# Reordering an attention-plus-gated-MLP kernel around its exponentials: layer norm statistics further ahead, the row-sum matmul moved to a later step, and seven eighths of the last output product moved forward

## The chip, the cores and the metric

One NeuronCore of a Trainium2 chip. The metric is the device time of one execution, in microseconds (us). Runs of this one-core program agree with the others of the same kernel within about 0.5%. The span of a profile is the time from the first to the last instruction of one profiled execution; it is some 2 us shorter than the time.

## The reference, cut to what matters

```python
x  = A_x                                   # 1 x 2048 x 512, bf16
xn = layernorm(x)
A  = softmax(q @ k.T * 16**-0.5) @ v, all heads, @ wo     # 32 heads of 16
B  = (relu(xn @ W_gate) * (xn @ W_up)) @ W_down           # hidden width 1792
out = x + A + B
```

Layer norm, attention and the gated MLP read the same normalized tensor. The softmax needs 32 x 2048 x 2048 exponentials.

## The kernel before

The kernel has three stages.

*Layer norm.* 16 tiles of 128 rows. For each tile VectorE sums the row and ScalarE sums the squares; for each chunk of four tiles a chain of tiny VectorE operations and one square root give mean and reciprocal deviation. Each tile is normalized in two passes on VectorE, transposed on PE through PSUM, copied to SBUF, and its V projection follows at once.

```python
for c in range(NQC):
    for i in range(4):
        t = 4 * c + i
        d_xn = ln_apply(t)                      # VectorE, two passes
        tk = transpose_tile3(t, d_xn)           # PE
        if prev is not None:
            pt_, ptk = prev
            evac_tile(pt_, ptk)                 # ScalarE for even tiles, VectorE for odd ones
            proj_V(pt_)                         # PE, then a copy on ScalarE
        prev = (t, tk)
        if i == 1 and c + 1 < NQC:
            for tt in range(4 * (c + 1), 4 * (c + 1) + 4):
                ln_stats(tt)                    # sum on VectorE, squares on ScalarE
        if i == 2 and c + 1 < NQC:
            rr = ln_finish_stats(4 * (c + 1), 4 * (c + 1) + 4)
```

*Attention.* A unit is one group of four heads with one chunk of 512 queries; there are 32 units, and 683 steps run through all of them. In each step PE makes three blocks of scores, ScalarE makes one exponential over 128 x 1536 of them, and PE multiplies earlier exponentials with V into one accumulator bank, psA (the row sums come from a column of ones in V). With what is left of a step PE does two matmuls of background work (the projections and the whole MLP, all through one bank, psX), or, when none is left, two idle "filler" matmuls. At a unit's end the accumulator is copied to `Tsb`, a matmul with a selection matrix (`sel`) spreads the row sums over the partitions, and VectorE and POOL divide.

```python
def emit_sel(u, dT):
    while st["psX_open"]:
        emit_bg_step()                          # finish the open background product in one burst
    pS = mm(psX[:], lhsT=sel[:], rhs=Tsb[:], start=True, stop=True,
            waits=[dT, g_sel] + psX_waits(), stream=s_peX)
    dL = vop(lambda: dve.tensor_copy(Lsb[:], psX[:]), waits=[pS, st["L_free"]])
    ...                                         # four reciprocal pieces, one per later step

for a in range(A_total + 1):
    ...                                         # scores, exponentials, PV; a unit's end emits the copy to Tsb
    emit_recip_piece()
    if pending_sel:
        emit_sel(*pending_sel.popleft())        # in the same step as the copy
        k = PE_BUDGET
    else:
        try_outproj()
        k = bg_advance(PE_BUDGET)
    for _ in range(PE_BUDGET - k):
        emit_filler()
```

*End.* After the last unit: copy, row sums, four reciprocals, one division on POOL, then the output product of the last 512 queries, 32 matmuls, and residual, and four writes.

The softmax here doesn't subtract the row's maximum and nothing guards it: scores larger than these inputs give would overflow.

## Time and profile before

| | before |
|---|---|
| time, median | 1099.17 us (16 runs, 1097.01 to 1100.65) |
| span of the profile | 1095.4 us |
| first exponential starts | 66.09 us |
| last exponential ends | 1075.73 us |
| time covered by exponentials | 981.0 us |
| idle of ScalarE between exponentials | 28.6 us |
| from the last exponential to the end | 19.7 us |

The span is the sum of four of these numbers: 66.1 before the first exponential, 981.0 covered by them, 28.6 between them, 19.7 after the last. Each is read from one profiled execution; that of the kernel before took 1097.41 us, 1.8 less than the median. The lines of the profile behind them stand in the prediction. In a row of the view in order of time the columns are start, length, engine, source line, operation, what is written and read, how many instructions were merged, and in brackets the idle time of the engine before it and what ended that. PE is the matmul engine (PEld its weight loads), DVE is VectorE, ACT is ScalarE, POOL is GpSimd.

### The profile page before, as it was taken

What the parts mean: (1) busy time and instruction counts of PE and PEld (TensorE: products, weight loads), DVE (VectorE), ACT (ScalarE), POOL (GpSimd) and SP (SyncE); (2) the same over time, 40 slices, a digit from 0 to 9 for tenths busy, and PEclk for the clock granted to TensorE, in tenths of its full rate; (3) what the DMA queues carried; (4) which work ended last, traced back from release to release, by engine and by line L of the source; (5) the groups of instructions that cost most, each with busy time, mean ns of one, the idle gap of its engine ahead of it and who ended that gap; (6) DMA issues with size and microseconds to landing.
All of it is one profiled execution on the core that took longest, in us unless ns stands there. A gap on an engine that the chain in (4) does not pass through costs nothing.

```text
span 1095.4 us, 13671 instructions
## 1 busy us (share of the span) xinstructions
PE 877.7 (80%) x5688; PEld 234.1 (21%) x5758; DVE 323.1 (30%) x498; ACT 1011.6 (92%) x746; POOL 49.2 (4%) x52
## 2 busy tenths in 40 slices
PE   3588888888888888888888888877778877777775
PEld 2222222222222222222222222221212222212211
DVE  5433323432332323443123342210112211101112
ACT  4479999999999999999999999999999999999992
POOL 1000010000000000000000000000000000000000
PEclk9789999999999999999999999999999999999998
DMA  9000000000000000000000000000000000000000
GB/s 335 1 1 1 1 7 15 1 1 1 1 1 1 20 1 1 1 1 1 1 1 1 21 1 1 1 1 1 1 1 1 20 1 1 1 1 1 1 1 20
DMA packets 8749, 12.67 MB, mean 12 GB/s; under 512 B 752, under 2 KB 7152, under 8 KB 8688
## 3 DMA queue, kind: packets, MB, share of 16 engines
q1 hardware_dynamic: 8688, 11.80, 3.1%
q8 instruction: 45, 0.74, 0.3%
q14 instruction: 16, 0.13, 0.0%
HBM read 9.70 MB, written 2.10 MB: 11 GB/s over the span
## 4 chain that ended last, share of the span: by engine, by line
ACT 50%; issue 22%; PE 18%; DVE 8%; DMA 1%; SPq 0%; POOLq 0%; POOL 0%; ACTq 0%
ACT PT L511 48%; PE psX L157 9%; PE psS L157 5%; PE psA L157 5%; DVE rl L576 2%; DVE Tsb L554 2%; DVE Lsb L564 1%; DMA W<-in_A_wqkv_dram 1%; ACT junk L216 1%; DVE hT L704 1%; DVE KTx L444 1%; DVE gl L686 1%; ACT Vsb L314 0%; DVE xpb L723 0%; DVE KTc L652 0%
## 5 line engine op out<-in xcount | busy, mean ns | idle before, releaser
L511 ACT ACTIVATE PT<-psS,negshift 128x1536 bf16<-128x1536 f32 (+1 forms) x683 | 981.0, 1606 | 33.4 <-PE psA L157 20.3
L157 PE MATMUL psS<-QT,KTx 32*128 32x512 bf16 x2048 | 268.5, 386 | 125.8 <-ACT PT L511 122.9
L157 PE MATMUL psA<-PT,Vsb 128*17 128x512 bf16 x2048 | 270.4, 386 | 0.5 <-ACT PT L511 0.5
L157 PEld LDWEIGHTS psS<-QT,KTx 32*128 32x128 bf16 x2048 | 66.5, 91 | 460.3 <-ACT PT L511 410.8
L157 PE MATMUL psA<-zmov,wfill 128*32 128x512 bf16 x462 | 138.0, 380 | 0.0
L554 DVE COPY Tsb<-psA 128x512 f32<-128x512 f32 x32 | 22.1, 692 | 318.3 <-PE psA L157 318.3
L576 DVE RECIPROCAL rl<-Lsb 128x128 f32<-128x128 f32 x128 | 113.5, 924 | 1.1
L157 PEld LDWEIGHTS psA<-PT,Vsb 128*17 128x17 bf16 x2048 | 64.0, 87 | 157.0 <-issue 155.6
L584 POOL TENSOR_TENSOR OT<-Tsb,rl 128x512 bf16<-128x512 f32 x32 | 40.6, 1268 | 1017.7 <-DVE rl L576 959.1
L157 PE MATMUL psX<-xnT,wu 128*128 128x512 bf16 x209 | 64.6, 384 | 7.7 <-DVE gl L686 2.7
L157 PE MATMUL psX<-xnT,wg 128*128 128x512 bf16 x205 | 64.0, 386 | 8.5 <-DVE hT L704 3.2
L686 DVE TENSOR_SCALAR gl<-psX 128x512 bf16<-128x512 f32 x56 | 38.5, 688 | 95.7 <-PE psX L157 95.6
L157 PE MATMUL psX<-wd,hT 128*128 128x512 bf16 x210 | 63.7, 384 | 3.3 <-issue 1.9
L704 DVE TENSOR_TENSOR hT<-psX,gl 128x512 bf16<-128x512 f32 x56 | 38.3, 684 | 88.4 <-PE psX L157 88.3
L157 PE MATMUL psX<-Tsb,sel 128*128 128x512 f32 x64 | 36.4, 652 | 27.2 <-DVE Tsb L554 15.0
L157 PEld LDWEIGHTS psA<-zmov,wfill 128*32 128x32 bf16 x462 | 40.3, 96 | 21.7
L157 PE MATMUL psX<-xnT,W 128*128 128x512 bf16 x104 | 33.7, 402 | 3.7 <-DVE KTc L652 1.4
L157 PE MATMUL psX<-W,OT 128*128 128x512 bf16 x94 | 30.0, 402 | 7.7 <-POOL OT L584 6.1
L564 DVE COPY Lsb<-psX 128x512 f32<-128x512 f32 x32 | 22.1, 692 | 40.6 <-PE psX L157 40.6
L723 DVE TENSOR_TENSOR xpb<-psX,xpb 128x512 bf16<-128x512 f32 x16 | 11.0, 690 | 77.7 <-PE psX L157 77.7
L157 PE MATMUL psS<-ident,xn 128*128 128x128 bf16 x64 | 8.8, 282 | 24.6 <-DVE xn L260 24.6
L603 DVE TENSOR_TENSOR ostage<-psX,xpb 128x512 bf16<-128x512 f32 x12 | 8.3, 692 | 52.8 <-PE psX L157 52.8
(72 smaller groups left out, 240.6 us busy)
## 6 DMA issues: line engine op xcount, KB each, us to landing
xpb<-in_A_x_dram SPq DMA_DIRECT2D x4, 512.0 KB, 5.5
wg<-in_B_W_gate_dram SPq DMA_DIRECT2D x1, 1792.0 KB, 14.1
wu<-in_B_W_up_dram SPq DMA_DIRECT2D x1, 1792.0 KB, 17.3
wd<-in_B_W_down_dram SPq DMA_DIRECT2D x1, 1792.0 KB, 21.0
W<-in_A_wqkv_dram SPq DMA_DIRECT2D x1, 1536.0 KB, 10.3
out_dram<-ostage SPq DMA_DIRECT2D x3, 512.0 KB, 3.0
W<-in_A_wo_dram SPq DMA_DIRECT2D x32, 16.0 KB, 1.7
out_dram<-ostage SPq DMA_DIRECT2D x4, 128.0 KB, 1.7
```

The costliest lines, as they stand in the source:

```text
L157: ins = pe.matmul(out_ap, lhsT=lhsT, rhs=rhs, start=start, stop=stop, **kw)
L216: a2 = aop(lambda: act.activation(junk[:], xt, ACTF.Square, accum_out=stats[:, 1, t:t + 1]), waits=[xload[t // 4], act_last[0]])
L444: tk = vop(lambda: dve.tensor_scalar(KTx[:, b, :], KTc[:, t8, :], msk[:, 0:1], None, op0=ALU.mult), waits=w)
L511: tk = aop(lambda: act.activation(PT[:, slot:slot + cnt, :].rearrange("p a q -> p (a q)"), psS[:, rb * 512:(rb + cnt) * 512], ACTF.Exp, bi ...
L554: dT = vop(lambda: dve.tensor_copy(Tsb[:], psA[:]), waits=[pv_tick, st["Tsb_free"]])
L564: dL = vop(lambda: dve.tensor_copy(Lsb[:], psX[:]), waits=[pS, st["L_free"]])
L576: dR = vop(lambda: dve.reciprocal(rl[:, k * wdt:(k + 1) * wdt], Lsb[:, k * wdt:(k + 1) * wdt]), waits=[dL, st["rl_free"] if k == 0 else None])
L584: gO = gop(lambda: pool.tensor_tensor(OT[:, g, :], Tsb[:], rl[:], ALU.mult), waits=w)
L603: d = vop(lambda: dve.tensor_tensor(ostage[:, tt, :], psX[:], xpb[:, tile, :], ALU.add), waits=[tk, xpb_ready[tile], out_dma_ticks[-1] if ...
L686: d = vop(lambda: dve.tensor_scalar(gl[:], psX[:], 0.0, None, op0=ALU.max), waits=[tk, bst["gl_free"]])
L704: d = vop(lambda: dve.tensor_tensor(hT[:, fc, :], psX[:], gl[:], ALU.mult), waits=w2)
L723: d = vop(lambda: dve.tensor_tensor(xpb[:, tile, :], psX[:], xpb[:, tile, :], ALU.add), waits=[tk, xload[c], ln_all_dve, ln_all_act])
```

## The change

It has three parts, one for each place where ScalarE is not making exponentials. In the layer norm, the statistics run two chunks ahead, one tile per iteration, the chain is cut in two around the square root, all transposed tiles are copied by VectorE, the square-root table is loaded at the start, and the setup on POOL is reordered. At a unit's end, the row-sum matmul is held back to a later step, when its operand has been copied and the bank psX is closed, and no burst is made. At the end, seven of the eight head groups of the last output product are summed beforehand into `oacc` with the residual, and the last group is divided and multiplied in four pieces.

```diff
@@ layer norm @@
-                if t % 2 == 0:
-                    e = aop(lambda: act.activation(xnT[:, :, t * 128:(t + 1) * 128], tp3, ACTF.Copy),
-                            waits=[tk, act_last[0]])
-                    act_last[0] = e
-                else:
-                    e = vop(lambda: dve.tensor_copy(xnT[:, :, t * 128:(t + 1) * 128], tp3), waits=[tk])
+                e = vop(lambda: dve.tensor_copy(xnT[:, :, t * 128:(t + 1) * 128], tp3), waits=[tk])
...
             for t in range(4):
                 ln_stats(t)
-            rr = ln_finish_stats(0, 4)
+            a3 = ln_chain_part1(0, 4)
+            if NQC > 1:
+                for t in range(4, 8):
+                    ln_stats(t)
+            rr = ln_chain_part2(0, 4, a3)
...
-                    if i == 1 and c + 1 < NQC:
-                        cn = c + 1
-                        for tt in range(4 * cn, 4 * cn + 4):
-                            ln_stats(tt)
-                    if i == 2 and c + 1 < NQC:
-                        rr = ln_finish_stats(4 * (c + 1), 4 * (c + 1) + 4)
-                        for tt in range(4 * (c + 1), 4 * (c + 1) + 4):
-                            r_ready[tt] = rr
+                    if c + 2 < NQC:
+                        ln_stats(4 * (c + 2) + i)
+                    if c + 1 < NQC:
+                        if i == 1:
+                            pend_a3 = ln_chain_part1(4 * (c + 1), 4 * (c + 1) + 4)
+                        if i == 2:
+                            rr = ln_chain_part2(4 * (c + 1), 4 * (c + 1) + 4, pend_a3)
+                            ...
@@ a unit's end @@
-                while st["psX_open"]:
-                    emit_bg_step()
+                assert not st["psX_open"]
...
-                if pending_sel:
+                if pending_sel and not st["psX_open"] and fix_at[0] < a:
                     emit_sel(*pending_sel.popleft())
                     k = PE_BUDGET
                 else:
-                    try_outproj()
-                    k = bg_advance(PE_BUDGET)
-                for _ in range(PE_BUDGET - k):
+                    if not pending_sel:
+                        try_outproj()
+                        try_preout()
+                    k = bg_advance(PE_BUDGET, allow_new=not pending_sel or fix_at[0] == a)
+                for _ in range(0 if fix_at[0] == a else PE_BUDGET - k):
                     emit_filler()
@@ the end @@
+            def last_piece(u, k, dR):
+                c_ = slice(k * 128, (k + 1) * 128)
+                ot_piece[k] = gop(lambda: pool.tensor_tensor(OT[:, g_of(u), c_], Tsb[:, c_], rl[:, c_], ALU.mult),
+                                  waits=[dR, st["rl_free"]])
...
+            def step_preout(qc, tt):
+                ...                             # groups 0 to 6 into psX, then
+                d = vop(lambda: dve.tensor_tensor(oacc[:, tt, :], psX[:], xpb[:, tile, :], ALU.add),
+                        waits=[tk, xpb_ready[tile]])
...                                              # the final product then takes group 7 alone and adds oacc
```

Left out of the diff: the setup on POOL in its new order and the table preload, the declarations of `oacc` and `junkb1`, the two halves of the statistics chain (their operations are unchanged), and the bookkeeping that starts the early output product two steps after the seventh group is divided.

## The prediction

> **What bounds the kernel now.** I read the page first (busy shares, then the costliest groups), then ScalarE's instructions in order of time with what ended each idle stretch, then all engines in order of time in three places: the layer-norm stage, one unit end of the attention loop, the end. A unit is one group of four heads with one chunk of 512 queries; there are 32.
>
> ```profile
> PE 877.7 (80%) x5688; PEld 234.1 (21%) x5758; DVE 323.1 (30%) x498; ACT 1011.6 (92%) x746; POOL 49.2 (4%) x52
> L511 ACT ACTIVATE PT<-psS,negshift 128x1536 bf16<-128x1536 f32 (+1 forms) x683 | 981.0, 1606 | 33.4 <-PE psA L157 20.3
> ```
>
> ScalarE is the bound, through 683 exponentials that cover 981.0 us. The change touches none of them, so the span can fall only where ScalarE is not doing exponentials: before the first (it starts at 66.09), in 33.4 us of idle time before them, and after the last (it ends near 1075.7; the span is 1095.4). Of the 33.4, 4.83 lie before the first, so 28.6 us are stalls inside the loop: 1075.7 - 66.1 = 1009.6 = 981.0 + 28.6.
>
> ScalarE in order of time shows where: runs of 21 or 22 exponentials, one unit long, with a stall between. In the stretch where the background work has run out the stalls repeat as 0.55, 0.56, 0.20; earlier many are 1.2 to 2.1. One of the small ones, all engines:
>
> ```profile
> 889.77 0.39 PE L157 MATMUL psS<-QT,KTx 32*128 32x512 bf16 x3 [0.29 <-ACT PT L511]
> 890.09 0.09 PEld L157 LDWEIGHTS psA<-PT,Vsb 128*17 128x17 bf16 x2 [0.23 <-issue]
> 890.53 0.69 DVE L554 COPY Tsb<-psA 128x512 f32<-128x512 f32 x1 [24.08 <-PE psA L157]
> 891.27 1.12 PE L157 MATMUL psX<-Tsb,sel 128*128 128x512 f32 x2 [0.79 <-DVE Tsb L554]
> 892.33 0.39 PE L157 MATMUL psS<-QT,KTx 32*128 32x512 bf16 x3
> 893.13 4.40 ACT L511 ACTIVATE PT<-psS,negshift 128x1536 bf16<-128x1536 f32 x3 [0.55 <-PE psA L157]
> ```
>
> The row-sum matmul (sel) is next in PE's order, so PE stands through the copy of the accumulator, spends 1.06 us on it, and the next scores begin at 892.33, 2.56 after the last instead of about 1.43. The exponential follows its scores by at least 0.44 (923.05 to 923.49 in another unit end). The 2 us stalls have one thing more: PE first finishes the open background product in one burst (seven matmuls from 256.65 and then a copy out) ahead of sel.
>
> The layer-norm stage:
>
> ```profile
> 32.05 0.17 DVE L223 TENSOR_SCALAR stats<-stats 128x4 f32<-128x4 f32 x1 [5.34 <-ACT junk L216]
> 33.46 0.20 ACT L235 ACTIVATE stats_b<-stats_b 128x4 bf16<-128x4 bf16 x1 [0.76 <-DVE stats_b L233]
> 34.56 0.61 PE L157 MATMUL psS<-ident,xn 128*128 128x128 bf16 x4 [5.07 <-DVE xn L260]
> 47.84 0.61 PE L157 MATMUL psS<-ident,xn 128*128 128x128 bf16 x4 [5.07 <-DVE xn L260]
> ```
>
> Each chunk of four tiles takes 13.3 us (21.3, 34.56, 47.84), because the squares of the next chunk stand in ScalarE's queue behind copies out of PSUM, VectorE's statistics chain stands behind the squares, and the tiles stand behind that. PE is idle 5 us per chunk.
>
> The end:
>
> ```profile
> 1078.85 3.39 DVE L576 RECIPROCAL rl<-Lsb 128x128 f32<-128x128 f32 x4
> 1082.31 1.26 POOL L584 TENSOR_TENSOR OT<-Tsb,rl 128x512 bf16<-128x512 f32 x1 [28.70 <-DVE rl L576]
> 1084.21 3.19 PE L157 MATMUL psX<-W,OT 128*128 128x512 bf16 x7 [6.12 <-POOL OT L584]
> 1087.19 5.42 PE L157 MATMUL psS<-W,OT 128*128 128x512 bf16 x24
> 1092.65 0.69 DVE L624 TENSOR_TENSOR ostage<-psS,xpb 128x512 bf16<-128x512 f32 x1 [1.04 <-PE psS L157]
> ```
>
> Everything here is serial, and 32 output matmuls hang on the last unit although only 4 of them read it.
>
> **The Trainium skill.** "TensorE: Matmul & The Clock Gate", Part 1, says the PE clock is halved until about 3.4 us of sustained activity, and again after an idle window of that length. The trace agrees: four projection matmuls take 1.87 us after each 5 us idle stretch (15.43, 21.87, 35.12) and 1.04 once PE has worked on (27.27, 40.55). The same page's queue depths call ScalarE and VectorE strict FIFO; the 5 us idle stretches are what that costs here. "ScalarE: Activation LUTs", What ACT_TABLE_LOAD costs, gives about 1283 ns for a load; the trace has 1.28 us at 0.73, 7.79 and 59.98. It gives 186 ns + 0.833 ns per element for an activation with immediates, 613 ns for 512; the trace has 0.60 for the copies, against 0.42 for the same copy on VectorE.
>
> **The change, part by part.**
>
> (1) *Layer norm.* Preloading the square-root table removes the load at 7.79, but that ended at 9.07, before the chain that it would delay (9.12): worth 0. The reordered POOL setup still has the identity by about 6 us, needed at 12: worth 0. Statistics now run two chunks ahead, one tile per step, so nothing waits for squares. Four reductions (2.46 us) come before the first tile: first transposes near 12.6 instead of 10.4, but the weights land at 13.1, so only about 1.2 us of it counts, V of tile 0 at 14.4. Then VectorE sets the pace: apply 0.65 and copy out 0.42 per tile, reduction 0.62 per tile in the first two chunks, statistics chain 7 x 0.20 + 0.2 = 1.6 in the first three. With about 0.05 more for the copies and starts: 8.2 + 8.2 + 5.7 us. In the last chunk PE paces at about 1.2 to 1.25 per tile (transposes at 54.70 and 55.89 in the old one, warm), 5.0. From the first apply at 11.85 that ends at about 39; allow 1.5 for the slow clock at the start. The last V product then starts near 41 instead of 58.24. I book 16 us rather than 17, since nothing has shown yet that PE stays at full clock at 60% load. The tail of this stage (key mean, first keys and queries, 7.85 us from that V product to the first exponential) is unchanged: first exponential at 50.
>
> (2) *Unit ends.* Sel moves to a later step, when the copy is done and psX is closed; no burst, and at the step of the fixup no filler waits for the copy. Sel now costs PE its 1.06 in a step that otherwise takes scores 0.32, PV up to 0.43 and a switch 0.23: 2.05 from one score start to the next, 2.15 or 2.25 if psX is just being copied out. Plus 0.44 gives at most 2.7, and the exponential is due two periods, 2.85, after the former score start. So the stall vanishes with 0.15 to 0.35 to spare. The next PV needs the accumulator copy: copy ends 0.75 + 0.69 after the fixup step's scores, PV comes 1.43 + 0.32 after: 0.3 to spare. Left of 28.6: 1.6 that are no unit ends (0.70 at the start, 0.70 near 356 to 362, 0.21 at 615) and an allowance of 2: 3.6 left, 25 saved.
>
> (3) *The end.* Seven eighths of the last output product plus the residual go into oacc in place of fillers. Steps: fix of unit 30 at step 668, start at 670, 28 matmuls at two per step through 683, the last step: they just fit. The final path: reciprocals to 1082.24 as before; a POOL piece of 128 columns about 0.5 (a 128x128 POOL operation took 0.54), so the last at 1082.8; four single matmuls; four adds on VectorE from 1082.3 at 0.70 each to 1085.1, instead of 1093.34. Saved 8.2, and the last write follows as before.
>
> Sum: 16 + 25 + 8.2 = 49.2; 1098.3 - 49.2 = 1049.
>
> **Rivals.** (a) *PE stays cold in the layer norm.* 16 tiles at 2.28 us from 14.4 would end near 51: 7 to 8 us saved instead of 16, time 1058. For: 60% load with a gap per tile. Against: gaps of 1 us from 25 to 28 did not slow it. (b) *The unit-end stall only moves.* Sel still takes PE 1.06, and if score starts slip past 2.4 or VectorE delays the copy, each unit keeps 0.2 to 0.3: 32 x 0.25 = 8 us, time 1057. Against: the 0.20 stall came at a spacing of 2.57 and fits 2.57 + 0.44 - 2.85 = 0.16. (c) *The early output product misses its slots* by a late sel of unit 30: then a burst after the loop, or the old ending, losing 2 to 8 us. (d) *Nothing gained*, background work being the real bound: no, from about 740 on PE runs fillers.
>
> **Range and chances.** Layer norm 8 to 18, loop 20 to 26.5, end 5 to 8.7; not all bad together: 1043 to 1058. Faster by over 2% (below 1076.8) needs 21.5 of 49: even the loop alone, or its low end with a little of the rest, does that. Faster 0.97, within 2% 0.025, slower 0.005.
>
> **What will show it.** First exponential near 50 (55 to 58: rival a, with 1.87 us projections throughout). Exponential busy still about 981. Idle before exponentials inside the loop 2 to 6 us; 0.2 after every unit end says (b). Sel with no wait on Tsb. From last exponential to end about 11.5 us instead of 19.7; four single output matmuls. Wrong altogether if the exponentials lengthen, or if ScalarE begins to wait for PE in the middle of units.

## The result

The changed kernel takes 1039.35 us (median of 8 runs, 1038.67 to 1041.3) against 1099.17; the ratio is 0.9461, with a 95% interval of 0.9451 to 0.947. A ratio here is the mean time of one kernel's fast runs over that of the other's of the same rounds, so it is not quite the ratio of the two medians. Between the medians 59.8 us are saved, between the two profiled executions below 58.2, since the one of the kernel before was faster than its median. The output is correct.

| us | before | after | saved | predicted |
|---|---|---|---|---|
| before the first exponential | 66.1 | 46.2 | 19.9 | 16 |
| idle between exponentials | 28.6 | 2.1 | 26.5 | 25 |
| covered by exponentials | 981.0 | 977.7 | 3.3 | 0 |
| after the last exponential | 19.7 | 11.2 | 8.5 | 8.2 |
| span | 1095.4 | 1037.2 | 58.2 | 49.2 |

The profile after, from the page: busy shares, and the group of the exponentials (count, busy time and mean length of one, then idle time before them and what ended it).

```profile
PE 855.4 (82%) x5595; PEld 224.3 (22%) x5669; DVE 327.3 (32%) x510; ACT 1002.4 (97%) x738; POOL 49.7 (5%) x55
...
L538 ACT ACTIVATE PT<-psS,negshift 128x1536 bf16<-128x1536 f32 (+1 forms) x683 | 977.7, 1948 | 7.0 <-PE psS L159 7.0
```

ScalarE is now busy 97% of the span. Of the 7.0 us of idle before exponentials 4.83 lie before the first one. The mean length is no measure of speed: it went up from 1606 to 1948 ns, while the same 683 cover less time. A listed length of an instruction runs into its successor's, and more so the less the queue pauses.

ScalarE in order of time, rows with a pause ahead of them:

```profile
54.41 279.17 ACT L538 ACTIVATE PT<-psS,negshift 128x1536 bf16<-128x1536 f32 x195 [0.36 <-PE psS L159]
333.79 244.83 ACT L538 ACTIVATE PT<-psS,negshift 128x1536 bf16<-128x1536 f32 x171 [0.20 <-PE psS L159]
578.83 389.37 ACT L538 ACTIVATE PT<-psS,negshift 128x1536 bf16<-128x1536 f32 x272 [0.20 <-PE psS L159]
```

Where the kernel before paused after every 21 or 22 exponentials, there are now runs of 195, 171 and 272. Three rows give the pitch: (389.37 - 244.83) / (272 - 171) = 1.431 us per exponential. The same pitch comes out before: its runs of 22 and 21 took 31.59 and 30.16. So the exponentials are no faster; there are only fewer interruptions. (The prediction names longer exponentials as a sign of being wrong altogether; by the pitch they are not longer.)

A unit's end with background work, all engines (weight loads left out):

```profile
80.34 0.39 PE L159 MATMUL psS<-QT,KTx 32*128 32x512 bf16 x3 [0.19 <-ACT PT L538]
...
80.66 0.60 PE L159 MATMUL psA<-PT,Vsb 128*17 128x512 bf16 x5
...
81.19 1.13 PE L159 MATMUL psX<-Tsb,sel 128*128 128x512 f32 x2
...
82.25 0.39 PE L159 MATMUL psS<-QT,KTx 32*128 32x512 bf16 x3
```

The row-sum matmul waits for nothing here; the spacing of the scores is 1.91 us (82.25 - 80.34) where it was 2.56, and ScalarE runs on through it. The prediction had allowed 2.05 to 2.25.

The layer norm, VectorE alone, one tile and the start of the next:

```profile
19.46 0.34 DVE L261 TENSOR_SCALAR xc<-xpb,stats 128x512 bf16<-128x512 bf16 x1
19.84 0.35 DVE L264 TENSOR_SCALAR xn<-xc,stats 128x512 bf16<-128x512 bf16 x1
20.11 0.41 DVE L296 COPY xnT<-psS 128x512 bf16<-128x512 bf16 x1
20.45 0.67 DVE L218 TENSOR_REDUCE stats<-xpb 128x1 f32<-128x512 bf16 x1
21.04 0.34 DVE L261 TENSOR_SCALAR xc<-xpb,stats 128x512 bf16<-128x512 bf16 x1
```

No row has a bracket: VectorE never pauses here. A tile takes 1.58 us from start to start, although the four lengths add up to 1.77. A chunk takes 7.8 us (tile 0 is begun at 11.63, tile 4 at 19.46) instead of 13.3. The last V product starts at 38.33 instead of 58.24.

The end:

```profile
1029.47 3.39 DVE L617 RECIPROCAL rl<-Lsb 128x128 f32<-128x128 f32 x4
1030.50 0.45 POOL L607 TENSOR_TENSOR OT<-Tsb,rl 128x128 bf16<-128x128 f32 x1 [25.16 <-DVE rl L617]
...
1032.77 0.63 DVE L691 TENSOR_TENSOR ostage<-psX,oacc 128x512 bf16<-128x512 f32 x1
...
1033.32 1.87 DVE L691 TENSOR_TENSOR ostage<-psS,oacc 128x512 bf16<-128x512 f32 x3
```

The pieces are divided while later reciprocals run, and the adds follow the last reciprocal without a pause. The early output product found its slots.

### The profile page after: what moved, and what is told of

Its sections match the earlier page's. It is cut to its first block, busy times and chain, and to the rows that moved or that the text cites. A ratio compares the mean times of both kernels' runs of the same rounds, so it can differ in the third digit from the quotient of the medians.

```text
span 1037.2 us, 13490 instructions
## 1 busy us (share of the span) xinstructions
PE 855.4 (82%) x5595; PEld 224.3 (22%) x5669; DVE 327.3 (32%) x510; ACT 1002.4 (97%) x738; POOL 49.7 (5%) x55
## 4 chain that ended last, share of the span: by engine, by line
ACT 48%; issue 27%; PE 17%; DVE 6%; DMA 0%; DVEq 0%; ACTq 0%
ACT PT L538 48%; PE psX L159 7%; PE psS L159 5%; PE psA L159 5%; DVE rl L617 1%; DVE Lsb L597 1%; DVE stats L218 1%; DVE hT L776 1%; DVE gl L758 1%; DVE KTx L471 1%; DMA xpb<-in_A_x_dram 0%; ACT junk L220 0%; DVE xn L264 0%; DVE xc L261 0%; DVE xnT L296 0%
## 5 line engine op out<-in xcount | busy, mean ns | idle before, releaser
L538 ACT ACTIVATE PT<-psS,negshift 128x1536 bf16<-128x1536 f32 (+1 forms) x683 | 977.7, 1948 | 7.0 <-PE psS L159 7.0
L159 PE MATMUL psA<-zmov,wfill 128*32 128x512 bf16 x373 | 111.5, 380 | 0.0
L617 DVE RECIPROCAL rl<-Lsb 128x128 f32<-128x128 f32 x128 | 110.7, 915 | 0.6
L795 DVE TENSOR_TENSOR xpb<-psX,xpb 128x512 bf16<-128x512 f32 x16 | 11.1, 691 | 118.6 <-PE psX L159 118.6
L159 PE MATMUL psX<-W,OT 128*128 128x512 bf16 x114 | 35.6, 384 | 3.7 <-DVE oacc L670 1.9
L159 PEld LDWEIGHTS psA<-zmov,wfill 128*32 128x32 bf16 x373 | 32.3, 96 | 17.0 <-issue 0.2
```

The source lines that it names most:

```text
L159: ins = pe.matmul(out_ap, lhsT=lhsT, rhs=rhs, start=start, stop=stop, **kw)
L538: tk = aop(lambda: act.activation(PT[:, slot:slot + cnt, :].rearrange("p a q -> p (a q)"), psS[:, rb * 512:(rb + cnt) * 512], ACTF.Exp, bi ...
L617: dR = vop(lambda: dve.reciprocal(rl[:, k * wdt:(k + 1) * wdt], Lsb[:, k * wdt:(k + 1) * wdt]), waits=[dL, st["rl_free"] if k == 0 else None])
L795: d = vop(lambda: dve.tensor_tensor(xpb[:, tile, :], psX[:], xpb[:, tile, :], ALU.add), waits=[tk, xload[c], ln_all_dve, ln_all_act])
```

## The experiments

Each ran on the chip beside the kernel before and was correct. "First", "idle", "covered" and "end" are the four terms of the span in that run's profile; "breaks" counts the pauses of more than 0.15 us between exponentials.

| run | time | ratio to before (95%) | first | idle | covered | breaks | end |
|---|---|---|---|---|---|---|---|
| before | 1099.17 | 1 | 66.1 | 28.6 | 981.0 | 35 | 19.7 |
| after | 1039.35 | 0.9461 (0.9451 to 0.947) | 46.2 | 2.1 | 977.7 | 5 | 11.2 |
| 1, layer norm alone | 1079.47 | 0.9822 (0.9806 to 0.9837) | 46.0 | 30.0 | 981.2 | 35 | 19.3 |
| 2, units' ends alone | 1068.40 | 0.9720 (0.9703 to 0.9737) | 66.1 | 3.9 | 978.0 | 7 | 19.7 |
| 3, end alone | 1089.34 | 0.9911 (0.9894 to 0.9929) | 65.3 | 29.2 | 981.5 | 36 | 10.9 |
| 4, sel in the same step | 1050.83 | 0.9563 (0.9543 to 0.9582) | 46.2 | 11.1 | 980.3 | 24 | 10.8 |
| 5, sel after a burst | 1054.06 | 0.9592 (0.9579 to 0.9605) | 46.1 | 14.6 | 979.6 | 15 | 11.2 |
| 6, even copies on ScalarE | 1046.66 | 0.9530 (0.9516 to 0.9545) | 54.2 | 0.4 | 978.0 | 2 | 11.2 |
| 7, old setup, no preload | 1040.09 | 0.9463 (0.945 to 0.9475) | 47.2 | 1.4 | 978.0 | 4 | 11.2 |
| 8, no early output product | 1049.04 | 0.9541 (0.9528 to 0.9554) | 46.1 | 3.7 | 978.2 | 6 | 19.1 |
| 9, old order of statistics | 1054.07 | 0.9583 (0.9558 to 0.9608) | 60.3 | 2.1 | 978.0 | 4 | 11.2 |
| 10, normalize in one pass | 1037.72 | 0.9435 (0.9414 to 0.9456) | 43.9 | 3.7 | 978.2 | 6 | 11.2 |
| 11, scores start early | 1037.39 | 0.9433 (0.9412 to 0.9454) | 44.1 | 1.4 | 978.0 | 4 | 11.2 |
| 12, 10 and 11 and one copy less | 1034.43 | 0.9405 (0.9383 to 0.9426) | 42.4 | 0.4 | 977.7 | 2 | 10.5 |

The four terms make the reading of each run simple, since nearly every edit moves one of them alone. One profile stands behind each row, and idle times differ by 1 to 3 us between profiles for a reason that is no part of the edits (see the slow stretches of PE, at the end of the part on the prediction).

**Runs 1 to 3: each part alone.** The edits take the other two parts back.

> Only the layer-norm part of the change, attention loop and end as before. Theory (the three parts add, each with the size read from the two traces): first exponential near 46.2 instead of 66.1, stalls inside the loop still 28.6 and exponential busy still 981, end still 19.7; time 1099.2 - 19.9 = 1079.3. Rival (interaction: part of the loop's gain is owed to the earlier start): more than 1 us away from that. On record in the prediction was 16 us, which would be 1083.2.

> Only the deferred row-sum matmul. Theory: stalls inside the loop fall to about 2 and the busy time of the exponentials falls from 981.0 to about 977.7, because an exponential that follows another without a pause overlaps its predecessor by about 0.11 and one after a stall does not; time 1099.2 - 29.8 = 1069.4. Rival (the 3.3 us of busy time come from elsewhere, the layer-norm part or the clock): busy stays 981, time near 1072.7.

> Only the early output product and the four pieces at the end. Theory: from the last exponential to the end 11.2 instead of 19.7, nothing else moves; time 1099.2 - 8.5 = 1090.7. Rival (the two early products that start in the middle of a step cost stalls in the loop): idle before exponentials up to 1 us more than 28.6 inside the loop, time near 1091.7.

The three alone save 1.78%, 2.80% and 0.89%, together 5.47%; the whole change saves 5.39%. The parts add, within the intervals, and each moves its own term: the first exponential comes at 46.0 with part 1 alone, the idle time goes from 28.6 to 3.9 with part 2 alone, the end shrinks to 10.9 with part 3 alone. Run 2 also places the 3.3 us of covered time: they come with part 2 (978.0, 7 breaks), and not with parts 1 or 3 (981.2 and 981.5 with 35 and 36 breaks). Run 3 took 1.4 us less than expected; 0.75 of it is the first exponential in its profile, which was earlier by that much without an edit there.

**Run 4: the row-sum matmul in the same step where psX is closed, but no burst.**

```diff
-                if pending_sel and not st["psX_open"] and fix_at[0] < a:
+                if pending_sel and not st["psX_open"]:
                     emit_sel(*pending_sel.popleft())
...
-                    k = bg_advance(PE_BUDGET, allow_new=not pending_sel or fix_at[0] == a)
-                for _ in range(0 if fix_at[0] == a else PE_BUDGET - k):
+                    k = bg_advance(PE_BUDGET, allow_new=not pending_sel)
+                for _ in range(0 if (fix_at[0] == a and pending_sel) else PE_BUDGET - k):
```

> The changed kernel, but the row-sum matmul may go in the same step as the accumulator's copy when psX is closed; if it is open the matmul still waits for it to close, so no burst. Theory (two causes of stall before: the wait for the copy, and the burst): the small stalls of 0.55, 0.55 and 0.20 come back at the unit ends with psX closed, up to 14 us of idle in all and fewer where psX is open, with lost overlap of 0.11 each; idle in the loop 9 to 16, busy 979.5 to 981, time 1048 to 1057. Rival (the burst was the whole cause): idle stays near 2 and the time near 1039.4.

ScalarE in order of time, late in the run, where there is no background work:

```profile
854.92 30.18 ACT L538 ACTIVATE PT<-psS,negshift 128x1536 bf16<-128x1536 f32 x21 [0.55 <-PE psA L159]
885.29 31.61 ACT L538 ACTIVATE PT<-psS,negshift 128x1536 bf16<-128x1536 f32 x22 [0.19 <-PE psS L159]
```

The old rhythm of 0.55, 0.55 and 0.19 is back at once, with runs of 21 and 22. The wait for the copy costs 9.0 us of idle (11.1 against 2.1; one pause of 1.82 in it falls into a slow stretch of PE), and with 19 more breaks the covered time is 2.6 longer.

**Run 5: a later step, but with the burst.**

```diff
-                if pending_sel and not st["psX_open"] and fix_at[0] < a:
+                if pending_sel and fix_at[0] < a:
+                    bg_finish_current()
                     emit_sel(*pending_sel.popleft())
```

> The changed kernel, with the row-sum matmul in the step after the accumulator's copy, but the open background product finished in a burst ahead of it, as before. Theory (the burst is the larger of the two causes, since taking back the same-step wait alone cost only 9 us of idle out of 26): idle in the loop 10 to 20 us, most of it in the first 22 units where there is background work and none worth a tenth after that; time 1049 to 1060. Rival (once the wait for the copy is gone the burst fits into PE's slack): idle under 6, time under 1045.

One of its pauses:

```profile
235.98 0.69 DVE L795 TENSOR_TENSOR xpb<-psX,xpb 128x512 bf16<-128x512 f32 x1 [2.56 <-PE psX L159]
...
236.73 1.12 PE L159 MATMUL psX<-Tsb,sel 128*128 128x512 f32 x2 [0.78 <-DVE xpb L795]
...
238.22 1.54 ACT L538 ACTIVATE PT<-psS,negshift 128x1536 bf16<-128x1536 f32 x1 [2.02 <-PE psS L159]
```

The background product is completed, PE waits for VectorE to copy it out of psX, and only then may the row-sum matmul have the bank. Idle is 14.6 us, 12.5 more than after. So the burst is the larger of the two causes. Of the 26.5 us that disappeared, the two together explain 21.5 one at a time; the other 5 appear only with both. Why is not shown. A delay may have to use up PE's slack in a step before it stalls ScalarE, and the slack can be used once; but the runs also do not restore the old order in full: where psX is open run 4 still holds the matmul back, and run 5 makes its burst a step later, when the step of the copy has already done some of it.

**Run 6: even tiles copied by ScalarE again.** The edit is the first hunk of the diff, taken back.

> The changed kernel, with the copies of the even transposed tiles back on ScalarE. Theory (VectorE paces the layer norm, it has no idle time there between 4.8 and 36.8): VectorE loses about 0.35 us for each of 6 tiles in the first three chunks, so the first exponential comes 1 to 2 us earlier than 46.2, time 1037.4 to 1038.4. Rival (ScalarE's queue order, which was the trouble before): the copy waits behind a square and a V copy, the tile chain lengthens and the first exponential comes 1 to 5 us later, time 1040 to 1044.

My theory failed here, and the rival was too mild: the first exponential comes 8.0 us later.

```profile
18.61 0.60 ACT L318 ACTIVATE Vsb<-psA 128x512 bf16<-128x512 f32 x1 [0.88 <-PE psA L159]
...
20.00 0.60 ACT L297 ACTIVATE xnT<-psS 128x512 bf16<-128x512 bf16 x1
...
20.65 1.04 PE L159 MATMUL psX<-W,xnT 128*128 128x512 bf16 x4 [1.43 <-ACT xnT L297]
```

PE ended the transposes and sums of tile 2 at 16.8. The copy of the tile (20.00) stands in ScalarE's queue behind the V copy of tile 1 (18.61), which had to wait for PE, and a square. Then PE waits for the copy, 1.43 us. Engines that each have slack still take turns when they hand the same tile to each other twice in one iteration. VectorE's saving of some 2 us is of no use to that chain. Not all of the 8.0 need be the queue's: PE's granted clock was half from 25.7 to 29.2 in this profile, and a like stretch cost 1.1 us in run 7.

**Run 9: the old order of the statistics, with all copies on VectorE.** The other corner of the two by two; the edit takes back the last two hunks of the layer norm, and the setup.

> The changed kernel, with the layer norm in its old order (squares and sums of the next chunk together, after its second tile) but all transposed tiles copied by VectorE. This closes the two by two: both old 66.1, only the statistics ahead 54.2, both new 46.2. Theory (the squares still stand behind the first V copy of the chunk and gate the next one; the copy shortens only the way to them): first exponential 60 to 64, time 1053 to 1057. Rival (the two add): 66.1 - 8.0 = 58.1, time 1051.

| first exponential at | even copies on ScalarE | all copies on VectorE |
|---|---|---|
| statistics of a chunk together | 66.1 | 60.3 |
| statistics two chunks ahead | 54.2 | 46.2 |

The statistics are worth 11.9 or 14.2, the copies 5.8 or 8.0: 20 us that part 1 saves are some 13 from the first and some 7 from the second, and the two nearly add. Run 9 fell where its theory had it. The prediction named the queue as the cause and sized both in one sum, without telling them apart. PE's clock is mixed into these numbers: between 25.8 us and the first exponential it was half for 13.7 us in the profile of the kernel before (32.6 to 39.4 and 46.3 to 53.1), for 10.2 in that of run 9, for 3.4 in that of run 6, and never in that of the changed kernel. What part of the differences this makes was not separated.

**Run 7: without the table preload and the new order on POOL.** The edit restores the setup of the kernel before.

> The changed kernel without the preloaded square-root table and with the POOL setup in its old order. Theory (the load at 7.8 ended before the chain that it would delay): first exponential within 0.2 of 46.2, time within 0.5 of 1039.4. Rival (the load now stands before the squares of tiles 4 to 7 and delays them): up to 1.3 us later, time 1040.7.

The ratio is 0.9463 against 0.9461; the two intervals cover each other. These edits have no effect on the time that these rounds can show. In the profile the first exponential was 1.1 us later, as far off as the rival said, but not for the rival's reason: up to tile 8 the two profiles agree within 0.06 us (it is begun at 27.05, against 27.10), and the whole delay arises in tiles 8 to 11, which take 6.4 us instead of 5.4. There PE's granted clock was half from 24.7 to 28.2, and VectorE waits 0.33 us for PE's transposes and then 0.66 for ScalarE's squares:

```profile
29.09 0.42 DVE L294 COPY xnT<-psS 128x512 bf16<-128x512 bf16 x1 [0.33 <-PE psS L159]
...
30.18 0.17 DVE L320 TENSOR_SCALAR stats<-stats 128x4 f32<-128x4 f32 x1 [0.66 <-ACT junk L218]
```

So the trace speaks for the clock in that execution as the cause of the delay, and not the setup; no second profile was taken to confirm it.

**Run 8: without the early output product.**

```diff
-                        try_preout()
```

> The changed kernel without the early output product; the last unit's four pieces stay, the 32 output matmuls are all at the end. Theory (both halves of part 3 count): the matmuls start when the first piece is there, 3 us earlier than in the kernel before, and then take their 9 us; from the last exponential to the end about 16.8 instead of 11.2, time 1045. Rival (the pieces are worth nothing without the early product): 19.7, time 1048.

```profile
1034.61 0.45 POOL L607 TENSOR_TENSOR OT<-Tsb,rl 128x128 bf16<-128x128 f32 x1 [0.36 <-DVE rl L617]
...
1035.32 3.57 PE L159 MATMUL psX<-W,OT 128*128 128x512 bf16 x8 [4.93 <-POOL OT L607]
```

The rival is right: the end takes 19.1 us. I had overlooked that without the early product the first output matmul also waits for the whole last unit, which is to say for the last of the four pieces. In that form the pieces alone give 0.6 us (19.7 to 19.1); the early product, on top of them, 7.9. What the pieces would give if each output tile waited for its own piece alone was not tried.

**Runs 10 to 12: where the layer norm ends next.** The readings above say that VectorE now paces the layer norm, and that after it the first scores wait for passes over all four key chunks. Run 10 normalizes in one pass:

```diff
-                d1 = vop(lambda: dve.tensor_scalar(xc[:, b2, :], xt, stats[:, 5, t:t + 1], None, op0=ALU.subtract), ...)
-                d2 = vop(lambda: dve.tensor_scalar(xn[:, b2, :], xc[:, b2, :], stats[:, 6, t:t + 1], None, op0=ALU.mult), ...)
+                d2 = vop(lambda: dve.tensor_scalar(xn[:, b2, :], xt, stats[:, 5, t:t + 1], stats[:, 6, t:t + 1],
+                                                   op0=ALU.subtract, op1=ALU.mult), ...)
```

> The changed kernel, with the two passes that normalize a tile (subtract, multiply, 0.35 us each) made one on VectorE; the intermediate rounding to bf16 falls away. Theory (VectorE paces the layer norm): 16 passes of 0.33 less, but in the last two chunks PE takes over at 1.19 a tile, so the first exponential near 42 to 43.5 instead of 46.2, time 1035.5 to 1037. Rival (PE and ScalarE pace it): first exponential not before 45.5, time 1038.5 or more.

The first exponential comes at 43.9, 2.2 us earlier and just outside what I expected: VectorE is the pace, but PE takes over sooner. The median time fell by 1.6 us, the profiled span by only 0.2, as this execution had 1.6 us more idle later on, in slow stretches of PE. Against the changed kernel the intervals touch (0.9456 and 0.9451), so for the time alone I don't call it shown.

Run 11 projects the queries first, sends the fourth key chunk to another bank, and writes the masked keys of the first unit in two parts, so that the first scores need one key chunk:

```diff
-            kslots = [bank(3), bank(4), bank(5), bank(2)]
+            kslots = [bank(3), bank(4), bank(5), psA[:]]
...
+                if qc == 0:
+                    ktx0[0] = vop(lambda: dve.tensor_scalar(KTx[:, 0, 0:512], KTc[:, 0, 0:512], mask_e[:, 0:1], None,
+                                                            op0=ALU.mult), waits=[kchunk_evac[0], g_masko])
```

> The changed kernel, with the first scores started when the first quarter of the keys is there: queries projected first, the masked keys of the first unit written as the first 512 columns and the rest, the last key chunk through the other bank. Theory (the 7.8 us from the last V product to the first exponential are a chain of VectorE passes over all four key chunks, of which the first scores need one): first exponential 42.5 to 43.5, up to 1 us of new stalls behind it, time 1036 to 1037.5. Rival (the exponentials only start earlier and then wait for the remaining chunks): first exponential earlier but 3 us more idle after it, time 1039.

The first exponential comes at 44.1, with no new idle behind it; less early than expected. Four VectorE operations in turn make the first quarter of the keys, ready at 42.28, and then the first scores, at 43.63, stand in PE's order behind the products of the other key chunks, the last of which starts at 42.67. For the time alone this run, too, is not clear of the changed kernel (0.9454 and 0.9451). Run 12 joins both and lets the reciprocals of the last unit read PSUM.

> Both of these, and the last unit's reciprocals read the row sums from PSUM without the copy of 0.7 us. If the gains add: 1039.4 - 3.2 - 2.7 - 0.7 = 1032.8, between 1031 and 1034.5. If VectorE's work after the layer norm is the next bound, the early start gains less on top of the fused pass: 1034.5 to 1036.

```profile
41.97 0.39 PE L159 MATMUL psS<-QT,KTx 32*128 32x512 bf16 x3
...
42.41 8.70 ACT L536 ACTIVATE PT<-psS,negshift 128x1536 bf16<-128x1536 f32 x6 [2.79 <-PE psS L159]
```

1034.43 us, ratio 0.9405 (0.9383 to 0.9426), clear of the changed kernel's 0.9451 to 0.947, and the lowest time, though its interval overlaps those of runs 10 and 11. The time lies at the border of the two expectations. At the first exponential the two gains don't add in full: 2.2 and 2.1 us, each alone, give 3.8 together; the copy left out gives 0.7 at the end, as expected. Run 10 and run 12 drop a rounding to bf16 that the reference makes; their outputs still passed as correct.

## Why the prediction was wrong, and where it was right

The direction and the mechanism of each part were right, the time was not: 1039.35 lies below the range of 1043 to 1058. The four terms add up to a span that is 9.0 us shorter than the sum in the prediction, and the errors all have one sign.

- **Part (1), the term "16 us", failed: it measured 19.9**, 3.9 of the 9.0. Run 1 shows the same with part 1 alone. The working had 58.24 to 41 for the last V product, 17.2 us, and booked 16; that haircut for an unproven clock is 1.2. The start of the last V product was 38.33 rather than 41, the other 2.7 are: 0.2 at the first apply (11.63), 0.4, 0.6 and 0.3 in the first three chunks (7.8, 7.6 and 5.4 us against 8.2, 8.2 and 5.7), and 1.2 behind them, mainly the allowance of 1.5 for the slow clock. In the profile of the changed kernel PE was slow until about 20 and then fast for the rest of the layer norm, and VectorE, which has the pace, paused only once between 8 and 36.8 us (0.42 us at 17.81, for ScalarE's square root). So rival (a) did not occur there; run 7 shows that PE's clock can still fall in this stage, at a cost of about 1.1 us.
- **The chunks were too long for one reason**: I added listed lengths, and these overlap. Apply, copy and sum of a tile came to 0.65 + 0.42 + 0.62 and 0.05 for starts, 1.74; start to start it is 1.58. The sum itself has a slip: four times 1.74 and 1.6 for the chain are 8.6, not 8.2, so added rightly it would have been further off. One reading is also wrong: the projection at 15.43 took 1.87 us, but PE had stood only 1.4 us before it began to work at 13.17, not 5; the ones at 21.87 and 35.12 do follow idle stretches, of 4.0 and 5.1.
- **"Exponential busy still about 981" failed: it measured 977.7**, 3.3 of the 9.0. The prediction took the covered time as a constant and the stalls as all there was to gain. But each exponential that follows another without a pause hides about 0.11 us behind it, and one after a pause does not: 981.0 with 35 breaks, 977.7 with 5, that is 3.3 / 30. At this rate run 4, with 24 breaks, should show 979.8 and run 5, with 15, 978.8; they show 980.3 and 979.6. None of the twelve experiments' profiles is further off than 0.8; all lie on the long side, for a reason not looked into. A stall costs its idle time and 0.11 on top, as the lengths of runs without a pause also say: 22 pitches of 1.431 are 31.48, the run took 31.59.
- **Part (2) was right in its mechanism, and slightly too careful**: 2.1 us of idle are left, not 3.6. The spacing of scores around the row-sum matmul was 1.91 and not 2.05 to 2.25. Rival (b), a fifth of a us left at each unit, did not occur; 0.2 is left at two places, neither a unit's end (PE waits 0.79 us there for VectorE to empty psX after an output product), and the rest of the 2.1 lies in slow stretches of PE. One piece of the reasoning is incomplete: its sum of spacing and 0.44 explains the stalls of 0.20, but those of 0.55 come at the same spacing, 2.56, and end with matmuls into psA (0.80 us after the start of the scores, in the lines shown).
- **Part (3) was right**: 8.5 against 8.2. Rival (c) did not occur.
- The worth of 0 for the table preload and the setup holds, by run 7: its layer norm starts its first tile at 11.57, against 11.63.

The range, too, was built from the parts' low and high ends one at a time, with high ends of 18, 26.5 and 8.7; their sum, 53.2, would have been 1045, so two of the three high ends were exceeded or reached and one error, the covered time, was no part of it.

**The slow stretches of PE.** Single pauses of 0.8 to 1.1 us (1.2 to 1.9 with the old order at the units' ends) come in some profiles and not in others. One of the changed kernel:

```profile
966.45 2.08 PE L159 MATMUL psX<-Tsb,sel 128*128 128x512 f32 x2
...
969.08 1.54 ACT L538 ACTIVATE PT<-psS,negshift 128x1536 bf16<-128x1536 f32 x1 [0.88 <-PE psS L159]
```

The row-sum matmul takes 2.00 us until the next scores (968.45), twice its usual 1.06. The profile also records PE's granted clock. In the view by stretches a row has the stretch, its length, the busy time and instructions of PE, its weight loads, VectorE, ScalarE and POOL, and at the end PE's mean granted clock, the share of DMA and GB/s:

```profile
54.10:965.40 911.30, 767.87 (x5017) 195.18 (x5081) 271.14 (x372) 910.58 (x637) 40.25 (x30) 1.00 0.01 3
965.45:968.87 3.42, 3.42 (x11) 0.74 (x11) 0.31 (x1) 2.75 (x2) 0.00 (x0) 0.50 0.00 0
```

PE ran at half clock from 965.45 to 968.87, and at full clock for 911 us before. The other stretch at half clock in this loop is 47.3 to 54.1, and the two early pauses (0.50 and 0.36 us) lie in it. The same holds for all profiles with the new order at the units' ends: outside stretches at half clock, of 3.4 or 6.8 us each, only 0.4 to 0.5 us of idle are left in the changed kernel and in runs 2 and 6 to 12. Run 12 had no such stretch in its loop and 0.4 us of idle; run 10 had three late ones, with pauses of 1.13, 0.88 and 0.81. The times of the changed kernel go with its mean granted clock: 1041.2 and 1041.3 us at 0.987, 1038.7 to 1039.8 at 0.990 to 0.992.

What sets off a slow stretch is open. This one begins just after PE stood 0.72 us in a unit's end whose step has no filler, but nine other unit ends of the same profile with that gap, and ten in run 12, brought none. The missing fillers are not needed for it: runs 1 and 3, which keep the fillers and the old order, have such stretches at 713.3, 1027.4 and 796.0, and the kernel before has one at 322.8, each after PE had stood about 0.8 us for the copy.

## What to carry to other kernels

When one engine is the bound, write the span as its time before, between, under and after its work, and size each term; then the parts of a change can be checked one by one. Take an engine's pace from start to start in a stretch without pauses, never from the sum of listed lengths, and count every pause on the bound engine twice: as idle time, and as lost overlap. If an in-order engine stands twice in one tile's chain, move one of the two steps to another engine, even to a busier one: here that gave 6 to 8 us for copies that VectorE could ill afford. And before an idle time is put down to an edit, look at the granted clock of that execution.

## What the Trainium skill lacked or had wrong

- "Perfetto Trace Analysis", Optimizing Scalar/DVE Operations, does say what I overlooked: the profiled latency is longer than the engine's busy time, as the write acknowledgement overlaps with the next instruction. It gives the overhead that is doubled in this way, 93 ns for ScalarE on SBUF and 51 on PSUM, but not the latency of an instruction; here a 128 x 1536 exponential with a pointer bias, which reads PSUM and writes SBUF, lists 1.54 us after a pause, and the pitch is 1.431; the four VectorE operations of a tile list 1.77 and pitch 1.58. No page draws the conclusion that each pause on the bound engine therefore costs more than its idle time (0.11 us here), though the overlap that the next point cites is of that size.
- "ScalarE: Activation LUTs", What ACT_TABLE_LOAD costs, gives 280 ns + 0.833 ns per element with a pointer bias and 93 ns of overlap back to back; an estimate from this for 1536 elements is 1560 - 93 = 1467 ns. The pitch here is 1431 ns, which over 683 exponentials is 25 us less. The page does not say whether its operand lay in SBUF or PSUM, and no run here separates the two.
- "TensorE: Matmul & The Clock Gate", Part 1, says that PE goes slow after an idle window of about 3.4 us. The changed kernel had PE at half clock for 3.42 us at 965.45, and the longest gap between matmuls in the 10 us before was 0.72; the page's section on a second failure mode tells of something similar with frequent short gaps, without the length of a gap.
